# Top-k attention into a gated two-layer block: paired search in the single slots, weights rounded three at a time, and another order in the paired slots

## The chip, the core and the metric

The kernel runs on one core of a Trainium2 chip. A core has a matrix engine (PE, with its weight loads listed as PEld), a vector engine (DVE), a scalar engine (ACT), a general engine (POOL) and a queue that mostly issues DMAs (SP). Each engine runs its own list of instructions in order, and semaphores make one wait for another. The metric is the device time of one execution in microseconds (us), as the median of several runs. All times below are in us unless they are marked otherwise.

## The reference

```python
scores = scale * np.matmul(q, k.transpose(0, 1, 3, 2))
kth = np.partition(scores, -top_k, axis=-1)[..., -top_k:-top_k + 1]
scores = np.where(scores >= kth, scores, -1000000000.0)
attn = np.exp(scores - np.max(scores, axis=-1, keepdims=True))
attn = attn / (np.sum(attn, axis=-1, keepdims=True) + 1e-09)
attn_out = np.matmul(attn, v)
...
h = x @ w_in
g = h * (1.0 / (1.0 + np.exp(-1.702 * h)))
return g @ w_out
```

q, k and v are 8 batches x 8 heads x 576 rows x 64, and top_k is 32. The heads of a row lie side by side as x, 4608 rows of 512. w_in is 512 x 2048 and w_out 2048 x 512. q, k and v are single precision; the two weights come as double precision and are rounded to single by the kernel.

## The kernel before

**Slots.** A slot is 128 rows of scores for a pair of heads (576 keys for each of the two). A batch has 18: four row blocks times four head pairs, and two slots that gather the 64 tail rows of the heads. 144 slots in all. In even batches the tail slots come last, in odd ones first. For each slot:

- `scores` (L317): PE writes two heads x 576 scores into four PSUM banks. There is one set of banks, so the next slot's scores wait until this slot's have been read. `copy_scores` (L332) copies them to SBUF on ACT.
- `topk` (L351): DVE finds the 32 largest of each row: four times the eight largest (MAX8, L363), with those removed in between (MATCH_REPLACE8, L367). That is 14 steps, two heads in each. In the paired form, `pair_up` (L341) first makes the larger and the smaller of each score and the one 288 places on. The first two rounds then look at the 288 larger ones only, and the last two at all 576. An unpaired search has 576 in every round.
- `bounds` (L376, POOL) makes the cut and the offset from the first and the 32nd largest. `mask` and `exps` (L391, L399, ACT) apply them. `invert` (L410) makes the reciprocal of the row sums.
- In the single slots `divide` puts the reciprocals on diagonals, and PE turns the weights with them (`turn`, L435), with ACT copying them out. In the paired slots `normalize` (POOL, L427) scales, `split` (ACT, L463) separates 16-bit halves, and two DMAs on SP write rows and read them back transposed into one of two tiles (`turn_by_dma`, L471).
- `values` and `values_at` multiply by v on PE. The result goes to x by an ACT copy (`x_of`, L543). When the last pair of heads of a row block is there, a block of 128 rows is ready for the second part.

**Blocks.** The second part takes each of 36 blocks in four units of four 128-wide slices of the hidden layer. A unit goes through `hidden` (PE, x times w_in), `tanh` (ACT, with a copy of h if the gate is put on POOL), `gate` (DVE or POOL), `combine` (sums of quarters) and `project` (PE). The first two blocks are whole (plain products). The others use seven products in place of eight, with sums of quarters of w_out that `weight_sums` makes on POOL (four groups, t1 to t4). After its fourth projection a block leaves PSUM by `leave_parts` (ACT, L715 to L719). Its parts are merged on POOL (`merge_some`, six items for a block) and written out when `write_all` puts the DMA on SP.

**Order.** Nothing is scheduled by a planner: the order of the calls is the order on each engine. `opening` loads, `slot(n)` runs slots 0 to 10 one by one, `first_pair(11)` two slots, and then `two_slots(n)` a pair at a time from slot 13. The first of these pairs, up to slot 20, are "filling": the second part starts there. The single slots also round the weights. Their 32 pieces of 128 x 512 come by DMA into a ring of seven places. `round_piece` (L135) gives each piece five steps: "size" (ACT, L158), "shift" (DVE, L159), "low" and "sign" (ACT, L161, L160) and two POOL steps (L151, L154), which must be done before the piece is used. Single slots 1 and 2 have a paired search, with the pairing at the end of the slot before. Slots 3 to 10 have an unpaired one, and from slot 11 on all are paired. Pairing reads both halves from SBUF up to slot 13 and the first half from PSUM after that.

In the steady pairs PE's order is: two hidden units, scores, two projections, values of two earlier slots, scores. `leave_all` stands at the end of the pair.

Of the kernel before, what the change touches and what calls it, by code (L numbers as in the profile page):

```python
# [30 lines left out]
def kernel(  # L31
# [55 lines left out]
    EARLY = (1, 2)  # L87
    by_pairs = lambda n: n in EARLY or PAIRED <= n < N
# [35 lines left out]
    raw = {}  # L124

    def load_piece(n):
# [5 lines left out]
        raw[n] = raws[:, n % RING, :]  # L132
        nc.sync.dma_start(raw[n], src.bitcast(U32))

    def round_piece(n):  # L135
# [8 lines left out]
        c, g = pieces[n]  # L144
        dst = wout[:, g, :] if c is None else win[:, c, g * PIECE : (g + 1) * PIECE]
        words = raw.pop(n).rearrange("p (n w) -> p n w", w=2)
        low, high = words[:, :, 0], words[:, :, 1].bitcast(F32)
        bits, whole = dst.bitcast(U32), dst.bitcast(I32)

        def add():  # L150
            nc.gpsimd.tensor_tensor(out=whole, in0=whole, in1=low.bitcast(I32), op=ALU.add)  # L151

        def finish():
            nc.gpsimd.tensor_tensor(out=dst, in0=dst, in1=high, op=ALU.mult)  # L154
            finished.append(None)

        return {
            "size": lambda: nc.scalar.activation(dst, high, AF.Abs, scale=REBASE),  # L158
            "shift": lambda: nc.vector.tensor_scalar(bits, bits, 3, None, op0=ALU.logical_shift_left),  # L159
            "sign": lambda: nc.scalar.activation(high, high, AF.Sign),  # L160
            "low": lambda: nc.scalar.mul(out=low.bitcast(I32), in_=low, mul=2.0**-29),  # L161
            "finish": [add, finish],
# [64 lines left out]
    def prepare_main(name, b, hp):  # L227
        src = loaded[b, hp]
        if name == "q":
            new_pair(b, hp)  # L230
# [7 lines left out]
    def turn_qk_ends(b, hp, ends):  # L238
        nc.tensor.transpose(ends, loaded.pop((b, hp))[1][:, 0, :, :], ident[:])
# [58 lines left out]

    def prepare_by_pe(b, hp):
        for name in "qk":  # L300
            prepare_main(name, b, hp)
        second_part.append((b, hp))
# [38 lines left out]
    def pair_up(n):  # L341

        sc = st[n]["sc"]
        a, b = sc[:, :, 0:HALF], sc[:, :, HALF:S]
        if n > PAIRED + 2:
            a = score_banks[:, :, 0, 0:HALF]
# [424 lines left out]
    by_slot = dict(enumerate([2, 2, 3, 3, 3, 3, 3, 3, 3, 3, 3, 1]))  # L771
    for n in by_slot:
        first = sum(map(len, list(by_slot.values())[:n]))
        by_slot[n] = list(range(first, first + by_slot[n]))
    assert by_slot[len(by_slot) - 1][-1] == NPIECE - 1
# [58 lines left out]
    def opening():  # L834
# [16 lines left out]
        early.extend(round_piece(x) for x in by_slot[0])  # L851
# [22 lines left out]
    def slot(n):  # L874
# [6 lines left out]
        some = [round_piece(x) for x in by_slot.get(n, [])] if n else early  # L881
# [4 lines left out]
        else:  # L886
            if not by_pairs(n):
                bounds(n - 1)
# [154 lines left out]
    def two_slots(n):  # L1043
# [37 lines left out]
        if live(n):  # L1081
            exps(n)
# [93 lines left out]
```

## Time and profile before

| what | us |
|---|---|
| median of the runs | 1414.6 (1413.47 to 1420.18) |
| the profiled execution | 1414.71 |
| its span in the profile | 1412.9 |
| busy in that span: PE, DVE, ACT, POOL | 1359.9, 1298.6, 1163.0, 967.3 |
| slot 8's search begins, DVE | 99.75 |
| slot 11's search begins (first pair) | 136.11 |
| slot 13's search begins (first steady pair) | 158.39 |
| slot 21's search begins | 238.73 |
| last search ends | 1347.1 |

The page gives the busy time of each engine, the span in 40 slices of busy tenths, the clock that PE was granted, the chain of work that ended last, and groups of instructions by line. The timeline gives single instructions: start, length, engine, line, what is written from what, and in brackets how long the engine stood idle before it and what ended that. The list of waits sums such idle time: who waited for whom, the sum, how often, the longest. Windows give the busy time of every engine in a stretch.

A slot's start is the first MAX8 of its search. By these starts, slots 1 to 10 take 9.88, 8.88, 12.37, 11.03, 11.50, 12.13, 11.60, 11.59, 11.79 and 12.98, and an undisturbed slot after that 8.63.

### The profile page before, as it was taken

What the parts mean: (1) busy time and instruction counts of PE and PEld (TensorE: products, weight loads), DVE (VectorE), ACT (ScalarE), POOL (GpSimd) and SP (SyncE); (2) the same over time, 40 slices, a digit from 0 to 9 for tenths busy, and PEclk for the clock granted to TensorE, in tenths of its full rate; (3) what the DMA queues carried; (4) which work ended last, traced back from release to release, by engine and by line L of the source; (5) the groups of instructions that cost most, each with busy time, mean ns of one, the idle gap of its engine ahead of it and who ended that gap; (6) DMA issues with size and microseconds to landing.
All of it is one profiled execution on the core that took longest, in us unless ns stands there. A gap on an engine that the chain in (4) does not pass through costs nothing.

```text
span 1412.9 us, 54415 instructions
## 1 busy us (share of the span) xinstructions
PE 1359.9 (96%) x22516; PEld 1214.5 (86%) x22516; DVE 1298.6 (92%) x3389; ACT 1163.0 (82%) x1896; POOL 967.3 (68%) x1740
## 2 busy tenths in 40 slices
PE   6779789999999999999999999999999999999998
PEld 5667468998988999899898999999998999999998
DVE  7999979999998999999999999999999999999922
ACT  6998678888879888888898988888888898888831
POOL 3788676767766777677776777777776777777740
PEclk8899899999999999999999999999999999999999
DMA  7452356787778778877887769777788877664540
GB/s 226 143 152 76 109 148 181 196 196 187 191 205 198 180 171 186 199 193 176 215 205 199 191 173 189 200 195 194 192 212 210 196 178 178 166 144 137 143 121 17
DMA packets 523831, 246.01 MB, mean 174 GB/s; under 512 B 455488, under 2 KB 502080, under 8 KB 523584
## 3 DMA queue, kind: packets, MB, share of 16 engines
q1 hardware_dynamic: 523152, 242.24, 68.7%
q8 instruction: 177, 2.90, 0.8%
q14 instruction: 70, 0.57, 0.1%
q10 hardware_dynamic: 432, 0.30, 0.1%
HBM read 45.09 MB, written 103.42 MB: 105 GB/s over the span
## 4 chain that ended last, share of the span: by engine, by line
PE 53%; DVE 19%; ACT 14%; issue 5%; POOL 5%; DMA 3%; SPq 1%; ACTq 0%; DVEq 0%; POOLq 0%
PE ph L594 21%; PE po L700 18%; DVE top L363 9%; PE o L534 6%; PE s_ps L326 6%; DVE ranked L367 5%; ACT pr L405 3%; ACT sc L467 3%; ACT sc L337 3%; DVE ranked L349 2%; DMA out_dram<-raws 2%; ACT sc L395 2%; DVE left L367 1%; POOL pr L431 1%; POOL th L623 1%
## 5 line engine op out<-in xcount | busy, mean ns | idle before, releaser
L363 DVE MAX8 top<-ranked 128x8 f32<-128x288 f32 (+1 forms) x1080 | 597.8, 596 | 0.0
L594 PEld LDWEIGHTS ph<-xT,win 128*64 128x64 f32 (+1 forms) x8736 | 478.9, 137 | 32.3 <-issue 18.9
L594 PE MATMUL ph<-xT,win 128*64 128x128 f32 (+1 forms) x8736 | 495.8, 274 | 3.5 <-ACT xT L548 3.5
L367 DVE MATCH_REPLACE8 ranked<-top,ranked 128x288 f32<-128x288 f32 (+1 forms) x810 | 433.7, 543 | 0.0
L467 ACT COPY sc<-pr 128x2304 uint16<-128x2304 uint16 x134 | 284.1, 2120 | 93.8 <-POOL pr L431 93.8
L431 POOL TENSOR_SCALAR pr<-pr,rden 128x576 f32<-128x576 f32 x268 | 197.2, 746 | 67.1 <-DVE rden L418 59.3
L405 ACT ACTIVATE pr<-sc,low 128x576 f32<-128x576 f32 x288 | 221.4, 780 | 0.0
L395 ACT ACTIVATE sc<-sc,cut 128x576 f32<-128x576 f32 x288 | 210.6, 792 | 4.8 <-POOL cut L381 4.7
L700 PE MATMUL po<-raws,h 128*64 128x128 f32 x2064 | 200.7, 273 | 2.4 <-POOL h L648 2.4
L700 PE MATMUL po<-wout,h 128*64 128x128 f32 x2064 | 201.0, 273 | 0.7
L349 DVE TENSOR_TENSOR ranked<-s_ps,sc 128x576 f32<-128x576 f32 x260 | 183.8, 749 | 18.3 <-ACT sc L337 18.1
L414 POOL TENSOR_SCALAR some<-den 128x2 f32<-128x2 f32 x132 | 29.1, 220 | 231.4 <-ACT pr L405 231.2
L326 PE MATMUL s_ps<-qk_t 64*64 64x288 f32 x2304 | 177.1, 421 | 7.4 <-ACT pr L405 6.1
L337 ACT COPY sc<-s_ps 128x576 f32<-128x576 f32 x288 | 171.1, 652 | 15.6 <-PE s_ps L326 12.6
L623 POOL TENSOR_TENSOR th<-th,h 128x512 f32<-128x512 f32 x131 | 167.7, 1280 | 10.9
L700 PE MATMUL po<-wout,th 128*64 128x128 f32 x2176 | 168.3, 276 | 0.0
L700 PEld LDWEIGHTS po<-wout,th 128*64 128x64 f32 x2176 | 124.6, 137 | 27.8 <-issue 9.7
L534 PE MATMUL o<-pt,v_l 128*64 128x128 f32 (+1 forms) x2400 | 144.0, 264 | 0.6 <-DMA v_l<-in_v_dram 0.5
L700 PEld LDWEIGHTS po<-raws,h 128*64 128x64 f32 x2064 | 130.1, 137 | 3.8 <-POOL h L648 3.8
L700 PEld LDWEIGHTS po<-wout,h 128*64 128x64 f32 x2064 | 129.9, 137 | 3.2 <-POOL h L649 3.1
L534 PEld LDWEIGHTS o<-pt,v_l 128*64 128x64 f32 x2400 | 126.8, 138 | 1.5 <-PE po L700 1.0
L326 PEld LDWEIGHTS s_ps<-qk_t 64*64 64x64 f32 x2304 | 75.9, 134 | 58.5 <-issue 21.0
(108 smaller groups left out, 1775.7 us busy)
## 6 DMA issues: line engine op xcount, KB each, us to landing
rows<-sc SPq DMA_DIRECT2D x134, 576.0 KB, 3.5
qk_rows<-halves SPq DMA_DIRECT2D x24, 576.0 KB, 5.2
out_dram<-raws SPq DMA_DIRECT2D x68, 128.0 KB, 3.6
raws<-in_moe_w_in_dram SPq DMA_DIRECT2D x16, 512.0 KB, 4.8
raws<-in_moe_w_out_dram SPq DMA_DIRECT2D x16, 512.0 KB, 3.5
qk_l<-in_q_dram SPq DMA_DIRECT2D x24, 256.0 KB, 4.4
qk_l<-in_k_dram SPq DMA_DIRECT2D x24, 256.0 KB, 4.4
v_l<-in_v_dram SPq DMA_DIRECT2D x4, 1024.0 KB, 6.5
```

The source lines that it names most:

```text
L326: nc.tensor.matmul(ps[rows, i, c, 0:HALF], lhsT=qT[b, hps[p]][on, cols], rhs=kT[b, hps[p]][on, FIRST[i] + c * HALF : FIRST[i] + (c + 1) * ...
L337: nc.scalar.copy(out=to, in_=ps[:, i, :, 0:HALF])
L349: nc.vector.tensor_tensor(out=ranked[n][:, :, c, :], in0=a, in1=b, op=op)
L363: nc.vector.max(top[:, i, 8 * r : 8 * r + 8], of(r, i))
L367: nc.vector.match_replace(to, top[:, i, 8 * r : 8 * r + 8], of(r, i), LOWEST)
L395: nc.scalar.activation(sc[:, i, :], sc[:, i, :], AF.Prelu, bias=cut[:, i : i + 1], scale=SCALE, alpha=HUGE)
L405: nc.scalar.activation(pr[:, i * S : (i + 1) * S], sc[:, i, :], AF.Exp, bias=low[:, i : i + 1], accum_out=den[:, i : i + 1],)
L431: nc.gpsimd.tensor_scalar(pr[:, i, :], pr[:, i, :], st[n]["rden"][:, i : i + 1], 1.0, op0=ALU.mult, op1=ALU.mult)
L467: nc.scalar.copy(out=halves, in_=pr[:].bitcast(U16).rearrange("p (k h) -> p h k", h=2))
L534: nc.tensor.matmul(o[j * D : (j + 1) * D, cols], lhsT=main[:, j, c, :] if c < NF else tail[:, j, :], rhs=pt[:, MAIN[j] + c if c < NF else ...
L594: nc.tensor.matmul(ph[rows, i * P : (i + 1) * P], lhsT=win[:, c, f * P + rows.start : f * P + rows.stop], rhs=xs[:, x.place, c, :], start= ...
L700: nc.tensor.matmul(both_banks[y * TAIL : (y + 1) * TAIL, bank, to * P : (to + 1) * P], lhsT=a[:, i, :], rhs=weight(w, fs[i])[:, y, :], sta ...
```

## The change

In the single slots every search but that of slot 0 is paired, and the pairing stands in the middle of the search before it (after eight of its 14 steps). It reads the first half of the scores from PSUM, there and in the first pairs. The weights of a slot are rounded together: three pieces in each slot from 1 to 10 (two in slot 0), so none is left for the first pair. One instruction does "low" for all three and one does "sign". "size" is done for two of the three on ACT and for the third on DVE ahead of the shift. The places in the ring are fixed: 0 to 2 for odd slots, 3 to 5 for even ones. The loads for the next slot are issued two steps of the search later. From slot 4 on, "low" stands ahead of the copies of the turned weights.

In the first pair the scores are made after the search, the weight sums begin there, and a projection stands ahead of the second search's end. In the filling pairs a second hidden unit is made from slot 15 on, the projection follows the search at once, the loads of batch 1 are turned at other places (`turn_mains`), and a block in parts is projected only when its weight sums have been issued. In all pairs the second projection stands behind the values in place of ahead of them, a block may also leave in the middle of the pair, and three merges are done at a time in place of two.

```diff
-    EARLY = (1, 2)
-    by_pairs = lambda n: n in EARLY or PAIRED <= n < N
...
-    def round_piece(n):
...
+    def round_pieces(ns):
...
+        def size():
+            for i, j in runs:
+                if i < 2:
+                    j = min(j, 2)
+                    nc.scalar.activation(home(i, j), high[:, i:j, :], AF.Abs, scale=REBASE)
+
+        def shift():
+            if len(ns) > 2:
+                nc.vector.tensor_scalar(home(2, 3), high[:, 2:3, :], REBASE, None, op0=ALU.mult)
+            for i, j in runs:
+                bits = home(i, j).bitcast(U32)
+                nc.vector.tensor_scalar(bits, bits, 3, None, op0=ALU.logical_shift_left)
+
+        def add(i):
+            whole = home(i, i + 1).bitcast(I32)
+            nc.gpsimd.tensor_tensor(out=whole, in0=whole, in1=low[:, i : i + 1, :].bitcast(I32), op=ALU.add)
+
+        def finish(i):
+            dst = home(i, i + 1)
+            nc.gpsimd.tensor_tensor(out=dst, in0=dst, in1=high[:, i : i + 1, :], op=ALU.mult)
             finished.append(None)
...
             "sign": lambda: nc.scalar.activation(high, high, AF.Sign),
             "low": lambda: nc.scalar.mul(out=low.bitcast(I32), in_=low, mul=2.0**-29),
-            "finish": [add, finish],
+            "finish": [lambda i=i, fn=fn: fn(i) for i in range(len(ns)) for fn in (add, finish)],
         }
...
+    mains = []
+
+    def turn_mains():
+        while mains:
+            for name in "qk":
+                prepare_main(name, *mains[0])
+            mains.pop(0)
+
     def prepare_by_pe(b, hp):
-        for name in "qk":
-            prepare_main(name, b, hp)
+        new_pair(b, hp)
+        mains.append((b, hp))
         second_part.append((b, hp))
...
         sc = st[n]["sc"]
-        a, b = sc[:, :, 0:HALF], sc[:, :, HALF:S]
-        if n > PAIRED + 2:
-            a = score_banks[:, :, 0, 0:HALF]
+        a, b = score_banks[:, :, 0, 0:HALF], sc[:, :, HALF:S]
...
-    by_slot = dict(enumerate([2, 2, 3, 3, 3, 3, 3, 3, 3, 3, 3, 1]))
+    by_slot = dict(enumerate([2, 3, 3, 3, 3, 3, 3, 3, 3, 3, 3]))
...
+        for i, x in enumerate(by_slot[n]):
+            place_in_ring[x] = (5 if n == 0 else 0 if n % 2 else 3) + i
...
-            if not by_pairs(n):
-                bounds(n - 1)
             exponentials(n - 1, bring_all if n % 4 == 1 and n > TURNS + 1 else lambda: None)
...
-            if i == (8 if n in EARLY else 5):
+            if i == 7:
+                pair_up(n + 1)
                 if n > 0:
                     divide(n - 1)
...
-        if by_pairs(n + 1):
-            bounds(n)
-            pair_up(n + 1)
+        bounds(n)
         for piece in some:
             piece["shift"]()
...
         if n >= TURNS:
+            for low in lows_of:
+                low()
+            lows_of = []
             turn_main(n - 1)
             turn_ends(n - 1)
...
     def project_one():
-        if may_project(0):
+        if may_project(0) and (to_project[0][3].whole or not summing):
             project(True)

     def first_pair(n):
...
         gate()
-        scores(n + 2)
         bring_all()
         exponentials(n - 1)
+        find(n, 10)
+        scores(n + 2)
         copy_scores(n + 2)
         leave_all()
         tanh(True)
         prepare_some()
-        some = [round_piece(x) for x in by_slot.get(n, [])]
...
         hidden(ps_t)
         project_one()
-        find(n, 10)
         normalize(n - 1)
         tanh(True)
         bounds(n)
...
+        summing.extend(weight_sums("t1", "b12", "b11") + weight_sums("t2", "b22", "t1") + weight_sums("t4", "b21", "t2"))
+        sum_weights(4)
         split(n - 1)
         begin(0)
         turn_by_dma(n - 1)
-        scores(n + 3)
+        leave_all()
         exponentials(n)
-        leave_all()
-        copy_scores(n + 3)
         find(n + 1, 10)
         project_one()
-        leave_all()
+        scores(n + 3)
+        copy_scores(n + 3)
         normalize(n)
...
         gate()
-        summing.extend(weight_sums("t1", "b12", "b11") + weight_sums("t2", "b22", "t1") + weight_sums("t4", "b21", "t2"))
+        sum_weights(4)

     def two_slots(n):
...
         if n == STEADY:
             prepare_some()
+            turn_mains()
         hidden(ps_t)
-        if n > STEADY + 2:
+        if n > STEADY:
             hidden(ps_t)
         tanh(aside)
         if n > STEADY + 4:
             prepare_some()
         combine()
-        merge_some(2)
+        merge_some(3)
         find(n, 8)
+        if filling:
+            project_one()
         if live(n + 2):
             scores(n + 2)
-        project_one()
+        if n == STEADY + 2:
+            prepare_some()
+            turn_mains()
+        if not filling:
+            project_one()
...
         combine()
-        merge_some(2)
-        project_one()
+        merge_some(3)
         sum_weights(4)
         if live(n):
             exps(n)
+        leave_all()
         tanh(aside)
...
         for what in ends:
             copy_qk_ends(*what)
+        turn_mains()
+        project_one()
         if filling:
             begin(1)
         find(n + 1, 8)
```

## The prediction

> **What bounds the kernel now.** I read the page's busy shares and slices first, to see where which engine idles.
>
> ```profile
> PE 1359.9 (96%) x22516; PEld 1214.5 (86%) x22516; DVE 1298.6 (92%) x3389; ACT 1163.0 (82%) x1896; POOL 967.3 (68%) x1740
> ...
> PE   6779789999999999999999999999999999999998
> ...
> DVE  7999979999998999999999999999999999999922
> ...
> PEclk8899899999999999999999999999999999999999
> ```
>
> PE is full from the sixth slice on; its idle time lies in the first 200 us, where DVE is full. DVE ends at 1347 us, and PE works on for 66 us. So the end is PE's work plus PE's idle time, and the early stages count by the idle time that they leave on PE. Windows (PE, PEld, DVE, ACT, POOL, clock, DMA) confirm it:
>
> ```profile
> 120.00:160.00 40.00, 34.47 (x259) 23.49 (x257) 39.87 (x92) 32.87 (x59) 28.53 (x31) 0.96 0.21 62
> 160.00:200.00 40.00, 32.74 (x238) 20.59 (x240) 34.15 (x90) 27.37 (x51) 29.77 (x42) 0.84 0.54 147
> ...
> 600.00:700.00 100.00, 99.21 (x1730) 89.93 (x1728) 94.51 (x251) 85.63 (x133) 70.86 (x135) 1.00 0.77 193
> ```
>
> A busy PE can still be late, so I took the score matmuls from PE's timeline as clock marks: those of slot 24 and of slot 142.
>
> ```profile
> 256.08 1.20 PE L326 MATMUL s_ps<-qk_t 64*64 64x288 f32 x16
> ...
> 1321.90 1.20 PE L326 MATMUL s_ps<-qk_t 64*64 64x288 f32 x16
> ```
>
> Between them lie 59 pairs of slots in 1065.82 us. An undisturbed pair takes 17.85 (9.58 + 8.27 between score marks: two hidden units 7.14, two projections 6.26, values 2.18, scores 2 x 1.13). 59 of them are 1053.15, so 12.7 us are lost. The waits and one such place say where:
>
> ```profile
> ACT raws L718 <- DMA out_dram<-raws: 41.0, 16, 7.1
> ...
> DVE ranked L349 <- ACT sc L337: 18.1, 11, 4.8
> ```
>
> ```profile
> 342.21 1.54 SPq L732 DMA_DIRECT2D out_dram<-raws  x2
> ...
> 346.00 0.98 ACT L718 ACTIVATE raws<-po 128x512 f32<-128x512 f32 x2 [1.28 <-DMA out_dram<-raws]
> ```
>
> A finished block leaves PSUM (L718) into a buffer whose previous content is still being written out; the score copies behind it on ACT come late, then DVE's pairing, then PE's scores. Of the 12.7 I put 10.8 on pairs next to such a wait (5.04 at 418 to 432 us alone) and 1.9 on others.
>
> **The change, part by part.** The profiled execution took 1414.71, its span 1412.9, so 1.8 lies around it; the median of the runs is 1414.6. The sum goes against 1414.7.
>
> *Slots 1 to 7.* A full search has 9.65 of its own (slot 8: 88.16 to 98.76, less invert 0.36 and gate 0.59), a paired one 7.25 (slot 18: 8.63, less pairing 1.32 and reciprocal 0.06). Pairing returns 1.32 of the 2.40. DVE also takes over one of three size steps: 0.33 by the step of L159, 0.59 by L625, also 512 elements; one shift over 1536 elements replaces three (0.33 each), 0.9. With gate 0.59 and inverse 0.27, DVE works 10.7 to 10.9 in slots 5 to 7, where they took 11.50, 12.13 and 11.60. ACT loses one size step (0.58) and some 0.1 per joined instruction: 10.0 of work, so DVE or a wait sets the slot.
>
> The wait that is added: pairing now stands eight steps into the search (3.15 after its start) and needs the score copies, which ACT makes behind mask 1.33 and exponentials 1.52, copies 1.05, all behind the cut.
>
> ```profile
> 98.76 1.08 DVE L159 TENSOR_SCALAR wout<-wout 128x512 uint32<-128x512 uint32 x3
> ...
> 98.94 0.98 POOL L381 TENSOR_SCALAR cut<-top 128x4 f32<-128x4 f32 x1 [1.45 <-DVE top L363]
> ```
>
> Here the cut took 0.98 because the shifts ran; it came 0.1 after the next search began, so copies would be ready at 4.1 and DVE would wait 1.0, with the rest of the search, the divide and six POOL steps behind it. While DVE ran L625 (74.61) the cut took 0.22; then it is early enough and the wait is nil. Slots 5 to 7 become 10.9 or 11.65 (before 35.2 together), slots 1 to 4 between 41.5 and 44.5 (before 42.16, with two slots paired already and one with two pieces). Together +3.2 to -2.3. The new step reads every second word, like neither row, so I take the middle: **+0.5**.
>
> Beside this: the ring has six places in use, not seven, so the loads for a slot wait for all three finishes of the slot before (POOL, 9.6 after its start); landing 3.7 later, 2.4 into the slot that needs them at 4.1. SP stands in that wait with later loads behind it, which have slots of time. Cost 0; with that cover gone, ACT's size step and the turned weights behind it come late. Slots 8 to 10 are bounded by PE (gapless 111.26 to 141.85), and nothing is counted there.
>
> *Filling, slots 11 to 20.* Counting units in the code: before, PE has done hidden units up to 11 and projected up to 10 when the scores of slot 20 end, at 220.93, 79.1 after that gapless stretch ends (141.85, "the mark"). After, the extra hidden unit of the second pair and the earlier projections make it 12 and 11: 3.57 + 3.13 = 6.7 taken from the tail. The work of PE to that mark, added up by its rows, is 68.3. Gapless would gain 17.5; all gaps kept, zero. Following the queues I find 11.4 of gaps: about 6 where values of slots 10 and 11 wait for their transposes (split ends 16 after the mark; in slot 11 of before, landing came 10 after the split), 5 in the next pair, where four PSUM users (two units, two turned loads) share two tiles and the second tanh comes only after the exponentials of slot 15. 68.3 + 11.4 = 79.7, so **+6.0** (6.7 - 0.6), ends 0 and 17.5. DVE waits too (5 at the inverse of slot 11, since ACT first empties block 0), but PE is busy then. A gain inside this:
>
> ```profile
> 139.26 3.54 DVE L349 TENSOR_TENSOR ranked<-sc 128x576 f32<-128x576 f32 x2
> ...
> 161.53 1.42 DVE L349 TENSOR_TENSOR ranked<-s_ps,sc 128x576 f32<-128x576 f32 x2
> ```
>
> Two pairings lose the slow form (2 x 2.1), and the weight sums (four groups of 4.97 on POOL) move one to two half-pairs earlier, where inverses still queue behind them.
>
> A rule stands behind these rows. The Trainium skill, SBUF — State Buffer, "Who interferes with whom", says that a DVE instruction with two SBUF inputs contends with GpSimd reads, and that a two-port tensor_scalar locks GpSimd out entirely; the first fits 3.54 against 1.42, the second speaks against the change, since a longer shift and one more tensor_scalar hold back the cut. By that rule the slots would be at their bad end and the time 2.8 higher than my sum; no row here has the strided step.
>
> *Steady pairs.* Three merges at a time finish the output one half-pair sooner, and the leave moves to the middle of the pair (one unit ahead shifts the block's end to the first projection). The write goes out behind the split of one pair, 12 before the next leave (331.6 against 343.6 in the pairs quoted); it lands in 3.6. **+10.8**, at least 5 if the queues stay crowded as at 410 to 419 us. On ACT the leave (0.87) now stands before a tanh; the split behind it waits 1.15 to 1.9 for POOL anyway. The second projection waits for the emptied bank, but values (2.18) lie between: 0.
>
> Losses, from moving values 3.13 forward on PE. (a) They now begin 11.3 after the pair's first hidden unit, the second one's at 12.4; its transposes land 8.4 to 14.0 after it, above 12.4 in seven pairs: -0.5, as SP gets earlier too: it issues a transpose only when values free its tile.
>
> ```profile
> 565.66 2.71 SPq L475 DMA_TRANSPOSE pt<-rows  x1
> ...
> 576.51 0.57 SPq L215 DMA_DIRECT2D v_l<-in_v_dram  x1
> ...
> 582.94 0.69 PE L534 MATMUL o<-pt,v_l 128*64 128x64 f32 x16 [0.48 <-DMA v_l<-in_v_dram]
> ```
>
> (b) Three times v arrives just as values start. It moves up by 2 of the 3.1: -2.0, at worst -9. (c) Being one unit ahead, both hidden units of every second pair need the newest xT, whose copy ends up to 1.46 late while DVE lags and in time once PE sets the pace: -1.7 once. (d) In the tail the last block's xT: -0.7. Together **-4.9**, ends -2 and -14.
>
> Sum: 0.5 + 6.0 + 10.8 - 4.9 = 12.4; 1414.7 - 12.4 = **1402.3**.
>
> **Rivals.** *Little gained:* the slots wait the full 1.0 and the filling keeps all its gaps: -2.3 + 0 + 5.9 = 3.6, 1411.1. For it: the search, mask, exponentials, copies and pairing form one loop of 11.65. Against: ACT has an idle microsecond per slot. *Slower:* in order on PE, values that wait hold up the second projection. The output's two issues (1.54) now stand between rows and transposes on SP; if transposes land 1.2 to 1.5 later in half the pairs, at 12.9 on average, PE waits 0.55 in 30 pairs, 17 us: 1419. It decides from 0.2 per pair on (12.4 over 61). Against it: SP waits about 3 there for rows to land. *More:* slots +3.2, filling +11, steady net +9: 1391.5. For it: the clock of 0.84 at 160 to 200 us, where PE ran at half speed beside its gaps.
>
> **How the numbers follow.** Forecast 0.55, little 0.18, slower 0.15, more 0.12. This kernel's measurement tells about 0.5% (7 us) from no change. Faster: 0.12 and 0.50 of the forecast, 0.62; same: 0.18 and a little of the rest, 0.20; slower 0.18. The range goes from the strong case to the slower one, 1391 to 1420.
>
> **What would show it.** Slots 5 to 7 at 10.9 or 11.65; DVE waiting for L337 in each of them or not; no 3.5 us pairing; L718 never waiting for out_dram; score marks 17.85 apart; one unit fewer after the last search. Wrong if values wait on pt or v in most pairs, or if the filling's ACT queue (turned loads, then split, then copies) delays pairing beyond what the extra unit returns.

## The result and the profile after

The changed kernel took 1422.1 us (median of 20 runs, 1418.5 to 1425.3). The kernel before took 1414.8 in as many runs beside it. The ratio is 1.0049, 95% interval 1.0038 to 1.0061. The change made the kernel about 0.5% slower, where 0.9% faster was forecast. The profiled execution of the changed kernel took 1420.9, with a span of 1419.0 (before: 1412.9).

The page of the changed kernel, busy times and three rows of the slices:

```profile
PE 1362.3 (96%) x22516; PEld 1216.7 (86%) x22516; DVE 1292.4 (91%) x3392; ACT 1159.1 (82%) x1835; POOL 966.8 (68%) x1746
...
PE   7679979999999999999999999999999999999998
...
DVE  7888878999999999999999999999999999999942
...
PEclk8799989999999999999999999999999999999999
```

PE runs the same 22516 matmuls as before, in 2.4 more; DVE is busy for 6.2 less and ACT for 3.9 less. What grew is idle time at the start: up to the scores of slot 24, PE stands idle for 47.9 (before 39.3) and DVE for 49.5 (before 23.7). From the eighth slice on PE is full, as before.

The score matmuls on PE serve as marks again. This table cuts both executions at the starts of the scores of slots 13, 20, 24 and 142:

| stretch | before | after | gained | forecast |
|---|---|---|---|---|
| start to slot 13 (single slots) | 141.85 | 153.71 | -11.9 | +0.5 |
| 13 to 20 (filling) | 77.95 | 83.47 | -5.5 | -0.6 |
| 20 to 24 (last filling pair, first steady) | 36.28 | 40.50 | -4.2 | 0 |
| 24 to 142 (59 steady pairs) | 1065.83 | 1056.19 | +9.6 | +6.6 |
| 142 to the end (one unit less) | 91.0 | 85.1 | +5.9 | +6.0 |
| span | 1412.9 | 1419.0 | -6.1 | +12.4 |

(The forecast for the steady stretch is 10.8 less the losses of 4.2 in it; that for the tail is 6.7 less 0.7. The column adds up to 12.5, since the prediction rounded 6.7 less 0.6 to 6.0. Before and after are spans of the profiled executions.) The steady pairs and the tail came out as forecast or better. The single slots lost 12.4 against the forecast and the filling 9.1, and that is the whole miss of 18.5 and 3.0 more, which the steady pairs gave back.

**Single slots.** DVE in the changed kernel, slots 6 and 7, with the searches left out (start, length, engine, line, operation, in brackets the idle time before it and what ended it):

```profile
95.46 0.47 DVE L167 TENSOR_SCALAR wout<-raws 128x512 f32<-128x512 f32 x1
95.97 0.96 DVE L170 TENSOR_SCALAR wout<-wout 128x1536 uint32<-128x1536 uint32 x1
...
101.62 1.42 DVE L379 TENSOR_TENSOR ranked<-s_ps,sc 128x576 f32<-128x576 f32 x2 [1.53 <-ACT sc L369]
```

POOL's cut, then ACT, in the same microseconds:

```profile
95.64 0.38 POOL L411 TENSOR_SCALAR cut<-top 128x4 f32<-128x4 f32 x1
```

```profile
96.03 1.67 ACT L184 ACTIVATE raws<-raws 128x1536 f32<-128x1536 f32 x1 [1.73 <-DVE wout L167]
97.58 1.43 ACT L425 ACTIVATE sc<-sc,cut 128x576 f32<-128x576 f32 x2
...
100.42 1.16 ACT L369 COPY sc<-s_ps 128x576 f32<-128x576 f32 x2
```

L184 is "sign". It overwrites the high words in place, and the third "size" step (L167, now on DVE at the end of the search) still has to read them. So "sign" for all three pieces starts only when DVE has finished the search and that step. ACT runs its list in order: mask (L425), exponentials and score copies (L369) stand behind it, and the pairing waits for the copies. The cut, which the mask also needs, was ready at 96.02; the mask began 1.56 later. DVE's waits for the copies in slots 1 to 7 are 1.02, 1.58, 1.35, 1.38, 1.15, 0.96 and 1.53, together 9.0. These slots took 87.2, before 77.4. DVE was busy for 77.7 of them, before for 76.0, and before it waited for no score copies there.

**Filling.** ACT in the pair of slot 15 (L643 copies a unit, L260 the turned loads of batch 1):

```profile
195.39 0.58 ACT L643 COPY h<-ph 128x512 f32<-128x512 f32 x1
203.44 0.58 ACT L260 COPY qk_t<-tp 128x512 f32<-128x512 f32 x1 [7.47 <-PE tp L259]
...
207.27 1.18 ACT L369 COPY sc<-s_ps 128x576 f32<-128x576 f32 x2
```

DVE, then PE, as a consequence:

```profile
208.49 1.42 DVE L379 TENSOR_TENSOR ranked<-s_ps,sc 128x576 f32<-128x576 f32 x2 [6.39 <-ACT sc L369]
```

```profile
212.80 2.07 PE L259 MATMUL tp<-ident,raws 128*128 128x128 f32 x8 [4.61 <-ACT h L643]
```

`turn_mains` puts the copies of the turned loads on ACT ahead of the split and the score copies. On PE the transposes for them (L259) stand behind two hidden units, a projection and the scores. ACT stood still for 7.5 with all of slot 16's work behind it. Slot 16 took 16.27 (before 11.34).

PE in the pair of slot 19, where the first block in parts leaves in the middle of a pair:

```profile
254.81 0.87 PE L730 MATMUL po<-wout,th 128*64 128x128 f32 x8 [2.62 <-ACT raws L748]
255.40 0.70 PE L730 MATMUL po<-raws,h 128*64 128x128 f32 x4
...
258.90 0.42 PE L730 MATMUL po<-raws,th 128*64 128x128 f32 x4
```

The leave (L748, the copy that takes a finished block out of PSUM) is on ACT behind the exponentials, and PE waits 2.62 for the emptied bank. Each group of four matmuls behind that takes 0.70 where 0.42 is usual: the projection took 4.94 where an undisturbed one takes 3.06. The granted clock was 0.85 from 248.5 to 260 and 1.00 on both sides of that. Wait and slow clock together are 4.5.

**Steady pairs.** The waits of the changed kernel from 290 to 1345 us (us in total, times, longest):

```profile
ACT sc L369 <- PE s_ps L358: 37.7, 59, 2.7
...
PE o L564 <- DMA v_l<-in_v_dram: 1.9, 1, 1.9
...
PEld o L564 <- DMA pt<-rows: 0.2, 1, 0.2
```

No line of the leave (L748) waiting for out_dram is left, against 41.0 before. ACT now waits for PE's scores: PE sets the pace.

### The profile page after: what moved, and what is told of

Read it like the earlier page. It is cut to its first block, busy times and chain, and to the rows that moved or that the text cites. A ratio compares the mean times of both kernels' runs of the same rounds, so it can differ in the third digit from the quotient of the medians.

```text
span 1419.0 us, 54280 instructions
## 1 busy us (share of the span) xinstructions
PE 1362.3 (96%) x22516; PEld 1216.7 (86%) x22516; DVE 1292.4 (91%) x3392; ACT 1159.1 (82%) x1835; POOL 966.8 (68%) x1746
## 4 chain that ended last, share of the span: by engine, by line
PE 87%; ACT 4%; DVE 2%; issue 1%; DMA 1%; POOL 1%; SPq 0%; DVEq 0%; ACTq 0%; POOLq 0%
PE ph L624 34%; PE po L730 29%; PE s_ps L358 10%; PE o L564 10%; PE po L715 2%; ACT pr L435 1%; ACT sc L369 1%; DVE top L393 1%; PE po L624 1%; ACT raws L184 1%; PE tp L475 1%; DVE ranked L379 1%; ACT sc L425 1%; DMA v_l<-in_v_dram 0%; DVE ranked L397 0%
## 5 line engine op out<-in xcount | busy, mean ns | idle before, releaser
L393 DVE MAX8 top<-ranked 128x8 f32<-128x288 f32 (+1 forms) x1144 | 633.0, 596 | 0.0
L397 DVE MATCH_REPLACE8 ranked<-top,ranked 128x288 f32<-128x288 f32 (+1 forms) x858 | 459.1, 543 | 0.0
L379 DVE TENSOR_TENSOR ranked<-s_ps,sc 128x576 f32<-128x576 f32 x286 | 202.0, 748 | 27.8 <-ACT sc L369 26.4
L369 ACT COPY sc<-s_ps 128x576 f32<-128x576 f32 x288 | 170.0, 644 | 60.3 <-PE s_ps L358 59.6
L425 ACT ACTIVATE sc<-sc,cut 128x576 f32<-128x576 f32 x288 | 209.1, 782 | 2.7 <-POOL cut L411 2.7
```

The source lines that it names most:

```text
L369: nc.scalar.copy(out=to, in_=ps[:, i, :, 0:HALF])
L379: nc.vector.tensor_tensor(out=ranked[n][:, :, c, :], in0=a, in1=b, op=op)
L393: nc.vector.max(top[:, i, 8 * r : 8 * r + 8], of(r, i))
L397: nc.vector.match_replace(to, top[:, i, 8 * r : 8 * r + 8], of(r, i), LOWEST)
L425: nc.scalar.activation(sc[:, i, :], sc[:, i, :], AF.Prelu, bias=cut[:, i : i + 1], scale=SCALE, alpha=HUGE)
```

## The experiments

All marks are starts of score matmuls, as in the table above. Ratios are to runs of the kernel before on the same chip, whose medians were 1415.3 to 1416.3. A stretch is read from one trace, and it scatters: in the seven kernels with the same filling pairs, 13 to 20 took 81.7 to 85.5.

### The old single slots with the new pairs

```diff
-    by_slot = dict(enumerate([2, 2, 3, 3, 3, 3, 3, 3, 3, 3, 3, 1]))
+    by_slot = dict(enumerate([2, 3, 3, 3, 3, 3, 3, 3, 3, 3, 3]))
...
     (before's slot(); first_pair(), two_slots(), turn_mains() of the change)
```

> The single slots of before (pairing only in slots 1 and 2, one instruction per piece, sizes on ACT; only the weight piece of slot 11 goes to slot 1) with the first pair, the filling and the steady pairs of the change. Marks are the starts of the score matmuls. Theory: the change lost 11.9 up to the scores of slot 13 in the single slots, and that loss is carried to the end; from there on it lost 5.5 up to slot 20 and 4.2 up to slot 24, won 9.6 up to slot 142 and 5.9 behind it. So this kernel has slot 13's scores at 141 to 144 and takes 1408 to 1411. Rival: the single slots' loss is not carried, since PE waits in the filling for something else; then slots 13 to 24 take up to 12 longer here than in the changed kernel and the time stays at 1417 to 1421.

1411.5, ratio 0.9973 (0.9958 to 0.9988). Slot 13's scores came at 142.7; then 82.3, 40.4, 1057.3 and 84.8. That is the theory, half a microsecond above its range: the loss of the single slots is carried to the end. Slot 13's scores come 11.0 sooner than in the changed kernel, and the time is 10.6 less. And the filling's losses are there without them. The pairs of the change alone make the kernel 0.3% faster.

### All size steps on ACT

```diff
         def size():
             for i, j in runs:
-                if i < 2:
-                    j = min(j, 2)
-                    nc.scalar.activation(home(i, j), high[:, i:j, :], AF.Abs, scale=REBASE)
+                nc.scalar.activation(home(i, j), high[:, i:j, :], AF.Abs, scale=REBASE)
...
         def shift():
-            if len(ns) > 2:
-                nc.vector.tensor_scalar(home(2, 3), high[:, 2:3, :], REBASE, None, op0=ALU.mult)
```

> The changed kernel with all three size steps on ACT, so that DVE has only the shift at the end of a search. Theory: ACT's sign step overwrites the words that DVE's third size step reads, so it can't begin before the end of the search, and mask, exponentials, score copies and the next pairing come late behind it. Without that DVE step sign begins 2 to 3 earlier, DVE's wait for the score copies falls from 1.0 to 1.6 to 0.9 or less per slot although ACT has 0.5 more work, and slots 2 to 10 take 11.3 to 11.6 in place of 12.4: slot 8's search begins at 100 to 103 (before 99.75, changed 109.27), the time is 1411 to 1414. Rival: the pairing waits for the chain of cut, mask, exponentials and copies whatever sign does; then only the DVE step itself (0.45 per slot) is saved and ACT's longer step gives some of it back: slots of 12.0 to 12.4, 1417 to 1421.

1416.1, ratio 1.0007 (0.9994 to 1.0021). Slots 7 to 9 took 11.46, 11.47 and 11.63, slot 8's search began at 103.7, slot 13's scores came at 147.6. Slots 7 to 9 follow the first theory, slots 2, 5 and 6 (12.29, 13.69, 12.04) do not. The time was 2 above the range. The profiled execution, 1419.3, was the slowest of the ten, 3.2 above the median; in it some of the gain was lost again behind the single slots (24 to 142: +4.0, half of it in the pair of slot 58, which took 4.2 too long in place of 2.3). POOL, ACT and DVE in slots 7 and 8:

```profile
102.96 0.90 POOL L407 TENSOR_SCALAR cut<-top 128x4 f32<-128x4 f32 x1
```

```profile
103.89 1.44 ACT L421 ACTIVATE sc<-sc,cut 128x576 f32<-128x576 f32 x2
```

```profile
107.94 1.42 DVE L375 TENSOR_TENSOR ranked<-s_ps,sc 128x576 f32<-128x576 f32 x2 [1.01 <-ACT sc L365]
```

The mask now starts with the cut, and a wait of 1.01 is left. That is the wait that the prediction had worked out from the cut behind the shift; what it had not seen is the part above it. Of the 0.96 that slot 7 gained, 0.53 is wait (1.53 to 1.01) and 0.41 is DVE's work (10.82 to 10.41), which the rival had named. Over slots 1 to 7 the wait fell from 9.0 to 7.4 and the work from 77.7 to 74.6.

### The third size step earlier on DVE

```diff
         def shift():
-            if len(ns) > 2:
-                nc.vector.tensor_scalar(home(2, 3), high[:, 2:3, :], REBASE, None, op0=ALU.mult)
...
+            if i == 9:
+                for piece in some:
+                    piece["third"]()
```

> The changed kernel with DVE's third size step ten steps into the search in place of at its end: the same work on every engine. Theory: sign waits for nothing, the pairing waits 1.0 or less per slot in place of 1.0 to 1.6, and slots 2 to 10 take 11.7 to 12.0: 4 to 6 less in all, 1415 to 1417. Rival: the place of the step does not matter, since the engines have the same work: slots of 12.4, 1420 to 1422.

1423.2, ratio 1.0062 (1.0047 to 1.0077): no gain, and above both ranges, so neither theory's numbers hold. But the wait did what the sign theory said: it is 1.01 in slots 6 and 7 in place of 0.96 and 1.53, and 9.6 in slots 1 to 10 in place of 13.7. What is left is mostly the cut. In the changed kernel ACT waited 13.8 in seven of these slots for DVE's third step; here it waits for the cut instead:

```profile
ACT sc L428 <- POOL cut L414: 12.6, 10, 2.6
```

What took the gain away is the step itself. POOL, then DVE:

```profile
102.43 1.29 POOL L180 TENSOR_TENSOR wout<-wout,raws 128x512 f32<-128x512 f32 x1
```

```profile
102.81 1.20 DVE L167 TENSOR_SCALAR wout<-raws 128x512 f32<-128x512 f32 x1
```

It took 1.20 in place of 0.47: it ends at 104.01, which is 0.29 after POOL's instruction (103.72). The same holds one slot earlier (90.28 + 1.20 = 91.48, POOL's ended at 91.20). So for most of that time it stood still, until POOL was done. Its mean over ten slots is 1.09, in the changed kernel 0.60. The Trainium skill, SBUF — State Buffer, "SBUF: two separate sides", says that the instruction that is first, a two-port DVE step or a GpSimd one, has the shared ports for its whole length and the other one blocks; these rows agree, and they show it with DVE as the loser. Which mode the step ran in, no row shows.

### Slot 4's sign in its own slot

```diff
-            if n == TURNS:
-                signs.append(piece["sign"])
-            else:
-                piece["sign"]()
+            piece["sign"]()
```

(on top of all sizes on ACT)

> The changed kernel with all sizes on ACT and, beyond that, slot 4's sign step in its own slot (the change puts off all of it to slot 5, behind the score copies). Theory: in slot 5 POOL waits 4.8 for that sign, so its steps run on to the end of the search, where the shift waits for them and the cut behind them; slot 5 falls from 13.7 to 11.3 to 11.8, and the time from 1416.1 to 1413 to 1415. Rival: something else makes slot 5 long (block work begins there), it stays above 13, and the time at 1416.

1415.2, ratio 0.9991 (0.9978 to 1.0005). Slots 5 and 6 took 12.84 and 11.44 (13.69 and 12.04 with all sizes on ACT alone), so 1.4 came back where 2 was expected, and slot 5 stays longer than its neighbours. In slot 5 DVE's work fell by 2.0 (12.46 to 10.49), but its wait for the score copies rose by 1.1 (1.19 to 2.31). The time is within a microsecond of the run before it, which the noise does not tell from no change: a small term, smaller than thought.

### The shift in the next search

```diff
         bounds(n)
         for piece in some:
-            piece["shift"]()
+            shifts.append(piece["shift"])
             unfinished.extend(piece["finish"])
...
         for i, op in enumerate(topk(n)):
             op()
+            if i == 1:
+                while shifts:
+                    shifts.pop(0)()
```

(on top of the last one)

> As the kernel with slot 4's sign in its own slot, and the shift stands behind the first two steps of the next search in place of at the end of its own. Theory: what is left of the pairing's wait (1.01) is the cut, which POOL makes while the shift runs (0.90 in place of 0.23), ahead of mask, exponentials, copies and pairing. With the cut alone it takes 0.2 to 0.4, the wait falls to 0.3 or less, slots 2 to 10 take 10.5 to 10.9 where PE does not bound them, slot 13's scores come at 138 to 142 and the time is 1405 to 1409. Rival: in its new place the shift meets POOL's steps, as the third size did in the middle of the search (1.20 in place of 0.45), or POOL's steps end too late for the next cut: slots of 11.3 to 12, 1413 to 1418.

1415.2, ratio 0.9998 (0.9982 to 1.0013), in the rival's range. The step was right and the sum wrong. POOL and DVE in slots 7 and 8:

```profile
99.12 0.23 POOL L407 TENSOR_SCALAR cut<-top 128x4 f32<-128x4 f32 x1
```

```profile
103.44 1.42 DVE L375 TENSOR_TENSOR ranked<-s_ps,sc 128x576 f32<-128x576 f32 x2 [0.41 <-ACT sc L365]
```

The cut takes 0.23, the wait falls to 0.41, and slots 7 and 8 take 10.79 and 10.80. So a paired single slot can be 0.8 shorter than the unpaired ones of before (11.60, 11.59). But slots 9 and 10 took 11.56 and 12.70, and slot 13's scores came at 143.3, not at 138 to 142. That is no earlier than with the old single slots. The profiled execution took 1412.8, the median was 2.4 above it. In slots 9 and 10 PE sets the pace, as before (11.79 and 12.98 there). Its scores in them begin at 108.33, 121.03 and 133.72, and in slot 10 it works for 11.80 of 12.70; what is left is a wait inside its own list:

```profile
133.36 0.44 PE L474 MATMUL tp<-by,pr 128*64 128x128 f32 x4 [0.90 <-ACT pt L479]
```

### The turned loads behind the score copies

```diff
-        if n == STEADY + 2:
-            prepare_some()
-            turn_mains()
...
         if live(n + 2):
             copy_scores(n + 2)
+        if n == STEADY + 2:
+            prepare_some()
+            turn_mains()
```

> The changed kernel with the loads of batch 1 turned behind the score copies in the pair that begins with slot 15, in place of ahead of the split. Theory: ACT stood idle 7.5 there (195.9 to 203.4) at a copy whose transposes PE makes only behind a hidden unit, a projection and scores, with the split, the score copies, the exponentials and the second tanh queued behind it; DVE lost 6.4 in slot 16 and PE 4.6 before the next unit. With the copies later, the 6.4 wait of DVE falls to 2 or less, PE's gap to 2 or less, the scores of slot 20 come 4 to 6 earlier after those of slot 13, and the time is 1414 to 1417. Rival: PE's work up to slot 20 sets the pace, and the gap reappears behind the transposes of slots 13 and 14: 1419 to 1422.

1417.6, ratio 1.0020 (1.0009 to 1.0030), half a microsecond above the theory's range, and 13 to 20 took 79.10 in place of 83.47. From 150 to 246 DVE waited for score copies:

```profile
DVE ranked L379 <- ACT sc L369: 3.6, 2, 2.0
```

The 6.4 is gone, the longest wait left is 2.0, and the stretch won 4.4: PE was idle for 2.2 less (10.4) and busy for 2.1 less (68.7), at a granted clock of 1.00 from 203 to 219 where it had been 0.79. So the copies' place on ACT was the cause of most of that loss.

### The steady part, taken apart

The steady edits on the kernel before, without the extra unit:

```diff
-        merge_some(2)
+        merge_some(3)
...
-        merge_some(2)
-        project_one()
+        merge_some(3)
+        if filling:
+            project_one()
...
             exps(n)
+        if not filling:
+            leave_all()
         tanh(aside)
...
             copy_qk_ends(*what)
+        if not filling:
+            project_one()
```

> The kernel before with the steady pairs of the change alone (values between the projections, a leave in the middle, three merges at a time), without the extra unit and the other edits of the filling. PE is then not one unit ahead, so a block still ends at the second projection and leaves at the end of a pair. Theory: what removes the wait of the leave for the write is that three merges put the write out one half-pair sooner, wherever the leave stands; the stretch from slot 24 to 142 takes 1055 to 1058 as in the changed kernel (before 1065.8), the time is 1404 to 1408. Rival: it is the leave in the middle of the pair, which needs the extra unit; then the stretch stays at 1064 to 1067 and the time at 1413 to 1417.

1425.4, ratio 1.0072 (1.0046 to 1.0098): slower than before, and outside both ranges. 24 to 142 took 1073.6, 7.8 more than before, in an execution of 1418.9, the fastest of the eight. The waits from 290 to 1345:

```profile
ACT raws L718 <- PE po L700: 65.5, 29, 3.6
```

No wait for out_dram is listed any more, so the earlier write does remove it, as the first theory said. But the block now ends at a projection that comes later by the values, its leave at the end of the pair waits for PE 29 times, 2.3 each, and the split and the score copies wait behind it. With the edits of the filling, the extra unit among them, the same three edits won 6 to 10 in this stretch; no run has the unit alone.

Two merges in place of three, in both places, in the changed kernel:

```diff
-        merge_some(3)
+        merge_some(2)
```

> The changed kernel with two merges at a time as before. Theory (the earlier write counts): the write now goes out in the very half-pair in which the next block leaves, the leave waits for out_dram again, and the stretch from slot 24 to 142 rises from 1056.2 to 1062 to 1070: 1427 to 1436. Rival (the place of the leave counts): the stretch stays at 1056 to 1058 and the time at 1420 to 1423.

1481.0, ratio 1.0478 (1.0434 to 1.0522); 24 to 142 took 1113.6, which is 57 more.

```profile
ACT raws L748 <- DMA out_dram<-raws: 41.1, 22, 5.2
...
PE po L730 <- ACT raws L748: 37.1, 22, 5.0
```

The direction of the first theory, but far beyond its 6 to 14. ACT waits for the write as long as before (41.0 there), but now it waits in the middle of the pair, with PE's second projection waiting for that very leave. A leave in the middle turns an ACT wait into a PE wait. PE stood idle for 39.4 more in this stretch and was busy for 18.1 more with the same work; the granted clock was 0.50 for 27 us of it, in the changed kernel at no time in it.

The second projection ahead of the values again, in the changed kernel:

```diff
         merge_some(3)
+        if not filling:
+            leave_all()
+            project_one()
         sum_weights(4)
...
-        project_one()
         if filling:
+            project_one()
             begin(1)
```

> The changed kernel with the second projection of a steady pair ahead of the values again, the leave being issued in front of it. Theory: the values (2.18 of PE) cover the leave, which stands on ACT behind the mask; without them PE waits 0.5 to 1.5 for the emptied bank in each of the 30 pairs where a block ends: the time is 1435 to 1465. Rival: the values' place does not matter for the leave, since ACT is done by then; PE gains a little where transposes or v come late (1.9 in the changed kernel): 1419 to 1423.

1463.0, ratio 1.0346 (1.0310 to 1.0381); 24 to 142 took 1096.8, 40.6 more.

```profile
PEld po L730 <- issue: 40.1, 29, 1.4
...
PE po L730 <- ACT raws L748: 33.9, 29, 1.2
```

PE waits 29 times, 1.2 each, for the emptied bank, as the theory had it. The values are the cover of the leave. The granted clock stayed at 1.00 through these short waits.

### Putting it together

The old single slots, the new pairs, the turned loads behind the score copies, and in filling pairs the leave ahead of the mask:

```diff
+        if filling:
+            leave_all()
         if live(n):
             bounds(n)
             mask(n)
```

> The single slots of before, the changed order of the pairs, and two moves in the filling pairs: batch 1's loads are turned behind the score copies in the pair of slot 15, and in filling pairs a block leaves PSUM ahead of mask and exponentials in place of behind them. Theory: the three losses are separate places, so the gains add. The order of the pairs with the old single slots took 1411.5; later turning took 4.4 out of the stretch from the scores of slot 13 to those of slot 20; in the pair of slot 19 PE stood 2.6 behind the leave, and the 4.94 of the projection after it would be 3.1. So that stretch takes 78, the one to slot 24 36 to 37 in place of 40.4, and the time is 1402 to 1404. Rival: one wait takes the place of another, and only the first or none of the two is gained: 1406 to 1411.

1406.1, ratio 0.9944 (0.9919 to 0.9969). 20 to 24 took 37.3 in place of 40.4, as expected: the leave behind the exponentials was the cause there. 13 to 20 took 81.7: only 0.7 of the 4.4 came, less than the scatter, and the time is in the rival's range (the eight runs took 1402.1 to 1409.8). The wait behind the turned loads is smaller, but PE was busy for longer with the same work (71.6 against 69.3 over 82 us), at a granted clock of 0.88 from 174 to 190, where the kernel without the two moves had 0.99.

Then also the second projection ahead of the values in the pair of slot 13:

```diff
+        if n == STEADY:
+            project_one()
         held = [m for m in (n - 3, n - 2) if live(m)]
...
-        project_one()
+        if n > STEADY:
+            project_one()
```

> The single slots of before with the changed pairs and the same three moves in them (1406.1 with two of them). Theory: the projection ahead of the values fills PE's wait of 4.2 for a transpose in the pair of slot 13, and the stretch from slot 13's scores to slot 20's goes from 81.7 to 77 to 78.5: 1401 to 1403. Rival: the projection is not ready by then, or the values that now come later hold up the hidden unit behind them: 1405 to 1408.

1402.4, ratio 0.9904 (0.9889 to 0.9919), and 13 to 20 took 77.4. The size is as expected, the reason only half. PE in the pair of slot 13:

```profile
170.27 1.98 PE L542 MATMUL o<-pt,v_l 128*64 128x128 f32 x16 [3.91 <-DMA pt<-rows]
```

The wait for the transpose is still 3.91 (4.16 without this move): the projection went in front, and the transpose came 2.3 later as well, counted from the scores. What is gained is that the scores of slot 16 no longer stand behind a projection that took 5.16 after the wait.

The same three moves on the kernel with the later shift:

> As the kernel with the later shift, and with three moves in the pairs: batch 1's loads turned behind the score copies in the pair of slot 15, the leave ahead of the mask in filling pairs, and the second projection ahead of the values in the pair of slot 13, where PE waits 4.3 for a transpose. Theory: all are separate places, so the time is that of the later shift less 7 to 11: 1396 to 1401. Rival: the pairs' waits replace each other as in the kernel that had two of these moves with the old single slots, where the stretch from slot 13 to 20 gained 0.7 in place of 4.4: 1402 to 1407.

1403.2, ratio 0.9910 (0.9895 to 0.9925), with 143.0, 76.3, 36.5, 1059.5 and 84.8. The three moves are worth 12 to it, more than the 7 to 11 of the theory, so here they do add; the time is in the rival's range because the kernel that they were put into took 1415.2 and not 1405 to 1409. The two kinds of single slots end within 2 us of each other (143.0 and 141.1). Windows from 200 to 240 us (PE, PEld, DVE, ACT, POOL busy, clock, DMA share, GB/s), first of the changed kernel, then of the one with the old single slots and three moves:

```profile
200.00:240.00 40.00, 34.04 (x492) 28.38 (x492) 25.54 (x67) 26.98 (x47) 21.23 (x35) 0.91 0.53 122
```

```profile
200.00:240.00 40.00, 40.00 (x738) 36.06 (x735) 33.93 (x88) 29.66 (x49) 23.67 (x44) 1.00 0.54 137
```

The second one is 18.7 us ahead there (its scores of slot 20 came at 218.5, against 237.2), and PE has no gap left in this stretch, at full clock. By their ratios both kernels beat the kernel before by 0.9 to 1.0% and the changed one by 1.4%.

## Why the prediction was wrong

**Slots 1 to 7 (+0.5 forecast, -9.8 measured): the step that failed.** The prediction listed "mask 1.33 and exponentials 1.52, copies 1.05, all behind the cut" and priced the pairing's wait at "nil or 1.0". The wait was never nil: it was 0.96 to 1.58 in each of these slots, 9.0 together. The prediction left "sign" out of that list, which stands on ACT ahead of the mask, and it did not ask who waits for the size step that is moved. It priced that step as DVE time (0.33 to 0.59; it measured 0.47 in slot 6, and DVE's work came out at 10.9, the forecast's upper value). The wait was 1.53 in slot 7; without the dependence 1.01, the forecast's bad end; with the cut freed from the shift 0.41. Those three runs show the cause of the wait piece by piece: without "sign" two thirds of it would be there all the same, from the cut behind the shift. The prediction had worked that part out and then taken the middle between its two ends; "sign" it had not.

Slots 5 to 7 were 14.03, 11.87 and 12.43, not 10.9 or 11.65. The bad end was also added up too low: three times 11.65 gives -2.1 in place of -2.3, but work 10.9 and wait 1.0 make 11.9, and three of those -2.8. The rival "little gained" had the right picture, one loop of search, mask, exponentials, copies and pairing, at a length that was too short.

Slots 1 to 7 in single traces, each kernel with the edits of the one before it:

| kernel | slots 1 to 7 | DVE's work | its wait for copies |
|---|---|---|---|
| before | 77.4 | 76.0 | 0 |
| changed | 87.2 | 77.7 | 9.0 |
| all sizes on ACT | 82.2 | 74.6 | 7.4 |
| and slot 4's sign in its own slot | 79.6 | 72.0 | 7.3 |
| and the shift in the next search | 77.7 | 72.4 | 5.1 |

The three edits return 9.5 of the 9.8, and more than half of that is DVE's work, not its wait. The paired slots then do less work than the unpaired ones and give it back as the wait that is left.

**Slots 1 to 4 (41.5 to 44.5 forecast, 48.9 measured).** The same waits, 5.3 together, which these slots didn't have before, and DVE steps stretched by POOL (a reciprocal's first step took 0.80 and 0.84 in place of 0.16). That POOL stretched them is argued from the rows: each ended within 0.05 of the end of a POOL instruction. Slot 5 was the longest: its three weight steps took 3.6 on DVE in place of 1.4, with POOL at work beside them, after POOL itself had waited 4.8 for slot 4's sign. Putting that sign back won 1.4.

**Slots 8 to 10 (nothing counted).** They were called bound by PE, gapless from 111.26 on. Once the loop of DVE and ACT took 12.4 to 12.6, it set the pace there too: 37.5 in place of 36.4, with PE busy for 33.9 of it, before for 33.7. A bound is one of the kernel before; the change moved it.

**Filling (+6.0 forecast, +1.2 measured on the same terms: 6.7 for the unit ahead, 5.5 lost).** The gaps that were named are there: 4.3 for the transpose (about 6 forecast) and 4.6 for the second tanh (5 forecast). The sign of being wrong "if the filling's ACT queue (turned loads, then split, then copies) delays pairing beyond what the extra unit returns" all but came true: 7.5 on ACT and 6.4 on DVE, against 6.7 for the unit. The sum was 68.3 of work and 11.4 of gaps; to the end of slot 20's scores PE was busy for 71.9 and idle for 12.7. So the term that was mis-sized is the work more than the gaps: it counted matmuls at full speed. The granted clock was 0.79 from 174 to 190 and from 203 to 219, and a projection after the wait took 4.25 where 3.63 is usual. The kernel before had shown as much, with 0.84 from 160 to 200.

**Emptied bank (0 forecast, -4.5).** "The second projection waits for the emptied bank, but values (2.18) lie between: 0" holds in the steady pairs (without the values it costs 40.6) and failed once, in the pair of slot 19, where ACT was late with its exponentials. Moving the leave won 3.2 to 4.0 there.

**Steady pairs and tail (right).** 10.8 was priced for the leave's wait, and it is gone; of the losses, v late cost 2.3 in the pair of slot 58 (2.0 forecast), late transposes 0.2 (0.5 forecast), the newest xT nothing that shows (1.7 forecast), and the tail is 5.9 shorter (6.0 forecast). The rival in which late transposes make PE wait in steady pairs gave 1419, near the time that came, by a mechanism that isn't in the trace.

**Range.** 1391 to 1420 missed the median by 2. The bad ends of the slots and of the filling were each in the text, but the slots' end (-2.3) was drawn from a wait whose cause was incomplete. That the time came so near the range's end is luck: the end stands next to the "slower" rival's time, and what that rival describes is not in the trace.

## What to carry to other kernels

When a step moves to another engine, list what overwrites its inputs, not only what reads its output, and look at what stands behind that writer in its own queue. A wait may be shorter than the chain that it starts: price every instruction ahead of the late one on each queue. A short step on DVE can take more than twice as long where POOL is at work (1.20 in place of 0.47 here). A stall of some 3 us on PE can cost more than itself, since the matmuls behind it run slow; 29 stalls of 1.2 left the clock at 1.00. Edits that pay only together (an earlier write, an earlier leave, work between, one unit ahead) have to be priced together: the kernels that lacked one of them lost 8 to 57 us in the steady stretch here.

## What was not expected of the hardware

- A DVE tensor_scalar between SBUF operands waited for the POOL instruction that was under way, to 0.29 after its end, in four places of two kernels (1.20 twice in the kernel with the earlier step, 1.05 and 1.38 in slots 4 and 5 of the changed one, in place of 0.47). The other way round POOL's cut took 0.90 under DVE's shift and 0.23 without it.
- An idle time of 2.62 on PE was followed by some 3.6 us of matmuls at 0.70 in place of 0.42. The Trainium skill, TensorE: Matmul & The Clock Gate, "What's actually happening", has the clock fall back after an idle window of some 3.4 us; here a pause shorter than that was enough, and the measurement decides. Windows of the changed kernel (PE, PEld, DVE, ACT, POOL busy, clock) show the stretch ahead of the fall and the one of the fall:

```profile
251.70:255.11 3.41, 0.79 (x24) 0.68 (x21) 2.93 (x7) 3.41 (x9) 0.93 (x2) 1.00 0.16 37
255.11:258.53 3.42, 3.42 (x37) 3.42 (x35) 3.42 (x9) 2.90 (x4) 3.24 (x7) 0.50 1.01 239
```

  In all fourteen traces, from 30 to 1300 us, the granted clock changes between 1.00 and 0.50 only at steps of 3.41. A step at 1.00 in which PE was busy for less than 1.4 was always followed by one at 0.50, one with more than 1.7 never. By that, where a pause lies on this grid can decide what it costs; no run tried it.
- In the other kernels with these steady pairs, they took up to 4 longer (1056.7 to 1060.2 against 1056.2), in the pair of slot 58, where most of them wait for v (2.0 to 4.2 too long there, 2.3 in the changed kernel), and in a few others. Most of these kernels came to the steady pairs sooner, but one came later and took 1058.1. Why v comes later in some stays open.
